# Moving loads, a small fold and the place of TensorE's instruction stream in a kernel that TensorE bounds

## The chip, the cores and the metric

The kernel runs on one core of a Trainium2 chip. The metric is the device time of one execution in microseconds (us). Engines are called PE (TensorE; its weight loads, PEld, are shown apart), DVE (VectorE), ACT (ScalarE), POOL (GpSimd) and SP (SyncE). L597 is line 597 of the kernel's source.

## The reference

Two steps, `mab` twice and then a two-layer network with a maximum. Four batches of 12,544 rows of 128 numbers go through both.

```python
def mab(q, kv):                       # attention, softmax over kv
    s = scale * (q @ kv.transpose(0, 2, 1))
    a = np.exp(s - s.max(-1, keepdims=True))
    a /= a.sum(-1, keepdims=True) + 1e-09
    return a @ kv
h = mab(I, x)                         # 32 inducing rows look at all of x
attn = mab(x, h)                      # all of x looks at the 32 rows of h
# then, with attn as rows of 128:
g = np.maximum(attn @ w1, attn @ w2)  # d_ff = 1024
out = g @ w_out
```

## The kernel before

The second `mab` and the network are fused. For each block of rows, PE makes the scores against `h`, ACT takes exp (tile `e2`), and **bursts** of eight small matmuls multiply it with `hwd` = h·(w2 - w1). DVE and ACT clip the results at zero into `relu`. **Finals**, 16 matmuls each, multiply `relu` with `w_out`, and DVE divides by the softmax sums into an output tile. The program is one list of 196 bursts, 49 a batch; after each burst comes one final, then whatever jobs are due at that burst:

```python
for g, (p, u) in enumerate(seq):
    # (cut: lead = opening products of two finals)
    p.burst(u, lead)                  # 8 matmuls, L597, and their evictions
    # (cut)
    for blk in stages.get(g, ()):
        blk.stage()                   # scores of a block that comes soon
    if queue:
        part, *a = queue.pop(0)
        part.final(*a)                # 16 matmuls, L659; every other one stores 256 KB
    # (cut: dens)
    for f, *a in jobs.pop(g, ()):
        f(*a)
```

The jobs of a batch prepare the next one: load its x, transpose it by DMA, make its scores and sums piece by piece (`p1_scores`, `p1_accum`), and at the end close the sum. `E`, the exponentials of the first `mab`, is summed into `eacc` on POOL, folded from 16 pieces to one, and PE adds it over the partitions:

```python
def small_fold(b):                    # four adds on POOL
    acc = st[b]["eacc"]
    n = P1B // 2
    while n:
        nc.gpsimd.tensor_add(out=acc[:, 0:n, :], in0=acc[:, 0:n, :], in1=acc[:, n : 2 * n, :])
        n //= 2
    st[b]["esum"] = acc[:, 0, :]

def small_h(b):                       # L413: the matmul that waits for it
    es = st[b]["esum"]
    bi, ps = bank([128, 512])
    nc.tensor.matmul(out=ps[:, 0:M], lhsT=ones32, rhs=es, start=True, stop=True)
    # (cut: DVE: reciprocal, hT4)

for b in range(B - 1):
    nb, g = b + 1, first[b]
    t0, l0 = (9, 24) if b == 0 else (-3, 16)
    at(g + t0, transpose_batch, nb)
    if nb + 1 < B:
        at(g + l0, hold_loads, nb)
    for i in range(NP1):              # 7 pieces
        s = g + (14 + 4 * i if b == 0 else 5 + 5 * i)
        at(s, p1_scores, nb, i)
        at(s + 2, p1_accum, nb, i)
        if nb + 1 < B:
            at(g + l0 + 3 * i, load_x, nb + 1, i)
    for s, f in ((41, small_fold), (43, small_h), (44, small_hwd), (45, small_m1)):
        at(g + s, f, nb)
```

POOL issues the loads (`load_x`) and most stores, and in its timeline the fold comes behind the store that the program puts ahead of it: in the profile before, at batch 2, that store went out at 169.85 us after 2.29 us of idle time that DVE ended, and the fold started at 170.41.

The softmax here doesn't subtract the row's maximum and nothing guards it: scores larger than these inputs give would overflow.

## Time and profile before

| | |
|---|---|
| time, 3 runs before the prediction | 341.23 us median (341.05 to 341.43) |
| profiled span | 339.1 us |
| PE busy | 329.4 us, 97% |
| DVE, ACT, POOL busy | 300.8, 270.7, 94.7 us |
| idle time of PE's matmuls over 0.15 us, after 40 us | 0.82, 0.76 and 0.76 us |

How to read it: PE is the engine that sets the time (97% busy, and 88% of the chain that ended last), so a microsecond counts only if it is taken from PE's own row. The prediction below shows the lines that lead to the three gaps. Two more ways of reading are used throughout:

- *Idle time with no releaser.* The profile ends a gap with the name of what released it. "<-issue" means that it found nothing. On a weight load, 0.2 to 0.4 us of "issue" is common here and cost nothing: in the profile before it stands 95 times ahead of the finals' weight loads (L659), 21.3 us in all and 0.4 at most, while their matmuls had no idle time (0.0 us).
- *Counting instructions.* Weight loads, matmuls and the few semaphore instructions of PE, counted in order of time, give each one its number. Whether two odd places are a multiple of 256 apart is then a subtraction. The 256 comes from the profile before: queue q8, which the page calls "instruction", moved 49 packets of 16,384 bytes, and PE's 12,646 records make 49.4 groups of 256. A packet that starts behind one crossing is read as holding what PE runs from the next crossing on: the two stalls of that profile ended 1.2 and 1.5 us after the end of packets that had started 3.7 and 4.4 us behind the crossings before them.

### The profile page before, as it was taken

To read this page: it belongs to the slowest core of one execution; us is meant where nothing else is said; L and a number is where in the kernel's file an instruction comes from. 1 tells how busy PE (TensorE), PEld (TensorE's weight loads), DVE (VectorE), ACT (ScalarE), POOL (GpSimd) and SP (SyncE) were. 2 spreads that over 40 slices of the span, in tenths; PEclk is the share of its full clock that TensorE was granted. 3 is DMA by queue.
4 is the path that set the end of the run, shared out by engine and by line. 5 is a ranking of instruction groups with operands and counts; after the bars stand their busy time and mean duration, and the time that the engine had idled before them with its cause. 6 is when DMAs were issued, how large, how long until landed. Compare 5 with 4: busy or idle time off the path is not lost.

```text
span 339.1 us, 14460 instructions
## 1 busy us (share of the span) xinstructions
PE 329.4 (97%) x6316; PEld 262.1 (77%) x6316; DVE 300.8 (89%) x634; ACT 270.7 (80%) x521; POOL 94.7 (28%) x166
## 2 busy tenths in 40 slices
PE   8999999999999999999999999999999999999995
PEld 3676788887878878888867878888767778878875
DVE  1669999999889999999988999999989998999993
ACT  3749878767898887888888877787879989888881
POOL 6332122437641233444242232333142100000000
PEclk9999999999999999999999999999999999999999
DMA  8999999999939985888319993221221221222223
GB/s 214 207 208 212 187 211 269 232 245 179 193 116 205 234 198 139 187 183 192 110 64 151 250 195 120 95 95 65 96 96 66 96 108 65 98 96 95 96 95 110
DMA packets 54143, 51.47 MB, mean 152 GB/s; under 512 B 41536, under 2 KB 42464, under 8 KB 54080
## 3 DMA queue, kind: packets, MB, share of 16 engines
q0 software_dynamic: 11552, 32.38, 38.1%
q1 hardware_dynamic: 42528, 18.17, 26.2%
q8 instruction: 49, 0.80, 1.0%
q14 instruction: 14, 0.11, 0.1%
HBM read 28.33 MB, written 25.69 MB: 159 GB/s over the span
## 4 chain that ended last, share of the span: by engine, by line
PE 88%; DVE 3%; DMA 3%; POOL 2%; ACT 2%; issue 1%; POOLq 0%
PE ps L659 55%; PE ps L597 19%; PE ps L612 4%; DMA xn<-in_x_dram 3%; PE ps L379 2%; PE ps L357 2%; PE ps L532 2%; ACT relu L632 1%; DVE relu L628 1%; DVE o L685 1%; POOL eacc L406 1%; PE ps L239 1%; PE ps L553 0%; PE ps L293 0%; PE ps L473 0%
## 5 line engine op out<-in xcount | busy, mean ns | idle before, releaser
L632 ACT ACTIVATE relu<-ps 128x512 f16<-128x512 f32 x443 | 234.6, 601 | 45.3 <-PE ps L597 30.8
L628 DVE TENSOR_SCALAR relu<-ps 128x512 f16<-128x512 f32 x341 | 219.6, 680 | 5.1 <-PE ps L597 4.2
L659 PE MATMUL ps<-woutp,relu 128*128 128x128 f16 x3136 | 208.7, 220 | 0.0
L659 PEld LDWEIGHTS <-relu 128*128 128x128 f16 x3136 | 175.7, 98 | 31.2 <-issue 21.3
L685 DVE TENSOR_TENSOR o<-ps,rp 128x256 f32<-128x256 f32 x196 | 82.0, 419 | 16.1 <-PE ps L659 11.2
L695 POOL DMA_DIRECT2D out_dram<-o x75 | 41.3, 551 | 156.7 <-DVE o L685 109.5
L597 PE MATMUL ps<-e,hwd 32*128 32x256 f16 (+1 forms) x1632 | 83.1, 268 | 1.6 <-issue 0.8
L597 PEld LDWEIGHTS <-hwd 32*128 32x128 f16 x1632 | 27.1, 92 | 20.7 <-issue 5.0
L612 PE MATMUL ps<-m,e 32*128 32x128 f16 x372 | 29.8, 214 | 0.7
L612 PEld LDWEIGHTS <-e 32*128 32x128 f16 x372 | 18.3, 92 | 6.8 <-issue 4.4
L399 POOL TENSOR_TENSOR eacc<-eacc,et 128x512 f32<-128x512 f32 (+1 forms) x18 | 18.5, 1030 | 0.3
L366 ACT ACTIVATE et<-ps 128x512 f16<-128x512 f32 (+1 forms) x21 | 11.4, 544 | 5.0 <-PE ps L357 5.0
L120 POOL DMA_DIRECT2D xn<-in_x_dram x21 | 11.4, 544 | 4.5 <-DMA xn<-in_x_dram 2.3
L542 ACT ACTIVATE e<-ps 128x512 f16<-128x512 f32 (+1 forms) x21 | 10.8, 568 | 0.0
L357 PE MATMUL ps<-inducingT,xT 128*128 128x32 f16 x294 | 10.6, 176 | 0.0
L379 PE MATMUL ps<-et,xn 128*128 128x32 f16 x294 | 10.6, 176 | 0.0
L357 PEld LDWEIGHTS <-xT 128*128 128x128 f16 x294 | 9.6, 96 | 0.0
L379 PEld LDWEIGHTS <-xn 128*128 128x128 f16 x294 | 9.5, 96 | 0.0
L532 PE MATMUL ps<-xT,hT 128*32 128x512 f16 (+2 forms) x120 | 8.7, 350 | 0.0
L191 PE MATMUL ps<-warm 128*128 128x512 f16 x22 | 7.4, 478 | 1.2 <-DVE warm L167 1.2
L239 PE MATMUL ps<-identity,xn 128*128 128x128 f16 x98 | 7.1, 219 | 0.6 <-DVE mask L726 0.3
L244 DVE COPY xT<-ps 128x1024 f16<-128x1024 f16 (+2 forms) x10 | 5.7, 585 | 1.4 <-PE ps L239 1.4
(84 smaller groups left out, 121.5 us busy)
## 6 DMA issues: line engine op xcount, KB each, us to landing
out_dram<-o POOLq DMA_DIRECT2D x72, 256.0 KB, 4.1
xn<-in_x_dram POOLq DMA_DIRECT2D x21, 512.0 KB, 8.5
out_dram<-o SPq DMA_DIRECT2D x24, 256.0 KB, 2.0
xf<-in_x_dram SPq DMA_DIRECT2D x2, 512.0 KB, 4.1
wf<-in_moe_w_dram SPq DMA_DIRECT2D x2, 512.0 KB, 5.0
xn<-in_x_dram POOLq DMA_DIRECT2D x3, 256.0 KB, 10.9
out_dram<-o POOLq DMA_DIRECT2D x3, 128.0 KB, 5.7
xT<-xn SPq DMA_TRANSPOSE x21, 7.0
```

Of the source, the lines that this page charges most:

```text
L120: nc.gpsimd.dma_start(out=xn_of(b, i)[:, 0:n, :], in_=xr[b, :, k0 : k0 + n, :])
L357: nc.tensor.matmul(out=ps[:, j * M : (j + 1) * M], lhsT=xT_tiles[b % 2][:, k0 + j, :], rhs=inducingT, start=True, stop=True,)
L379: nc.tensor.matmul(out=ps[:, 0:M], lhsT=xn[:, j, :], rhs=et[:, j, :], start=(j == 0), stop=(j == n - 1),)
L399: nc.gpsimd.tensor_add(out=acc, in0=acc, in1=et[:, 0:n, :])
L532: nc.tensor.matmul(out=ps[32 * q : 32 * (q + 1), 0 : self.width], lhsT=st[self.b]["hT4"][:, 32 * q : 32 * (q + 1)], rhs=xT[:, q % self.g], ...
L597: nc.tensor.matmul(out=ps[:, jj * w : (jj + 1) * w], lhsT=st[blk.b]["hwd"][r, 128 * jb : 128 * (jb + 1)], rhs=blk.e2[r, 128 * self.t0 : 12 ...
L612: nc.tensor.matmul(out=part.fin[q][1][:, 128 * s : 128 * (s + 1)], lhsT=part.blk.e2[r, 128 * tt : 128 * (tt + 1)], rhs=st[part.blk.b]["m1" ...
L628: nc.vector.tensor_scalar(out=dst, in0=src, scalar1=0.0, scalar2=None, op0=ALU.max)
L632: nc.scalar.activation(out=dst, in_=src, func=AF.Relu)
L659: nc.tensor.matmul(out=o, lhsT=self.relu[:, jb, q, tt, :], rhs=woutp[:, jb, :], start=(start and s == 0 and jb == 0), stop=(not start and ...
L685: nc.vector.tensor_mul(self.osb[:, h : h + 2, :], ps[:, 0:256].rearrange("p (s c) -> p s c", s=2), rp.broadcast_to((128, 2, 128)),)
L695: eng.dma_start(out=outr[blk.b, :, k : k + nst, :], in_=self.osb[:, 0:nst, :])
```

## The change

Its intent: end the loading of a batch sooner, take the fold of E out from behind a store, and put PE's instructions at a chosen place in the blocks in which they are fetched.

```diff
-                    at(g + l0 + 3 * i, load_x, nb + 1, i)
-            for s, f in ((41, small_fold), (43, small_h), (44, small_hwd), (45, small_m1)):
+                    at(g + l0 + 2 * i, load_x, nb + 1, i)
+            d = 1 if b == 0 else 0
+            for s, f in ((40, small_fold), (42 + d, small_h), (43 + d, small_hwd), (44 + d, small_m1)):
                 at(g + s, f, nb)
@@
         queue = []
+        nfinal = 0
@@
             if queue:
+                if nfinal == 4:
+
+                    nc.tensor.addr_align(256, offset=174, max_nops=0)
+                nfinal += 1
                 part, *a = queue.pop(0)
                 part.final(*a)
```

`addr_align(256, offset=174, max_nops=0)` asks that the next instruction lie at slot 174 of a block of 256.

## The prediction

> **What bounds the kernel now.** I read the page's busy rows first, then the waits, then the timeline at the places that the waits name. The page:

> ```profile
> span 339.1 us, 14460 instructions
> PE 329.4 (97%) x6316; PEld 262.1 (77%) x6316; DVE 300.8 (89%) x634; ACT 270.7 (80%) x521; POOL 94.7 (28%) x166
> ...
> PE   8999999999999999999999999999999999999995
> ...
> DMA  8999999999939985888319993221221221222223
> ...
> q8 instruction: 49, 0.80, 1.0%
> ```

> TensorE (PE) is busy in 97% of the span, and the slices show no hole of half a slice between the start and the last slice. The chain that ended last is 88% PE. So time can come only from PE: less work for it, which the change doesn't bring (its order of instructions gains one entry, the alignment), or fewer stalls. The DMA row shows two stretches of near full load, up to about 165 us, and light load after. I went through PE's matmuls in order and looked for idle time over 0.15 us. From 40 us to the end there are three: 0.82 us at 83.80, 0.76 at 172.47 and 0.76 at 251.30. The timeline shows what they are. The last two look alike; here is the second of them and, for comparison, the same place one batch earlier, where nothing waits:

> ```profile
> 91.53 1.99 POOL L406 TENSOR_TENSOR eacc<-eacc 128x256 f32<-128x256 f32 x4
> ...
> 93.77 0.30 PEld L413 LDWEIGHTS ps<-eacc,ones 128*128 128x128 f32 x2
> ...
> 169.85 0.54 POOL L695 DMA_DIRECT2D out_dram<-o  x1 [2.29 <-DVE o L685]
> ...
> 170.41 2.00 POOL L406 TENSOR_TENSOR eacc<-eacc 128x256 f32<-128x256 f32 x4
> ...
> 172.47 0.41 PE L413 MATMUL ps<-eacc,ones 128*128 128x32 f32 x2 [0.76 <-POOL eacc L406]
> ```

> The fold of E takes GpSimd (POOL) 2.0 us. At 170 us it stands in POOL's queue behind an output store that waits for VectorE (DVE), so it starts at 170.41 and PE waits for it. In the first batch it ends at 93.52 and PE comes at 93.77: no wait.

> The stall at 83.80 has no releaser. It falls inside a burst of eight matmuls, between the seventh and the eighth, where nothing in the program can differ:

> ```profile
> 82.59 0.39 PE L597 MATMUL ps<-e,hwd 32*128 32x256 f16 x7
> ...
> 83.80 0.09 PEld L597 LDWEIGHTS <-hwd 32*128 32x128 f16 x1 [1.10 <-issue]
> ...
> 83.80 0.28 PE L597 MATMUL ps<-e,hwd 32*128 32x256 f16 x1 [0.82 <-issue]
> ```

> A smaller one of the same look, also before the eighth of a burst, is in the weight loads at 70.86:

> ```profile
> 70.38 0.12 PEld L597 LDWEIGHTS <-hwd 32*128 32x128 f16 x7
> 70.86 0.09 PEld L597 LDWEIGHTS <-hwd 32*128 32x128 f16 x1 [0.36 <-issue]
> ```

> [...] With boundaries every 256 counted from these two, a fetch packet starts at or after each crossing: at once (within 0.2 us) for most crossings after 210 us, where DMA is light, but 3.7, 3.7 and 4.4 us late at the crossings of 64.80, 70.86 and 76.95 us. The packet then takes 0.9 to 1.5 us, and the stalled instruction came 1.2 to 1.5 us after its end. So a fetch under load needs about 3.7 to 4.4 + 0.9 + 1.3 = 5.9 to 6.6 us, while PE uses a block up in 5.9 to 7 us. That is the whole margin.
> [...]

> **The change part by part.**
> 1. *Fold of E one burst sooner.* For batches 2 and 3 the fold and all that follows (h, hwd, m1) move one burst forward; for batch 1 the fold alone. POOL's order becomes: store issued at 167.00, then the fold, at about 167.56 to 169.56, instead of after the store at 169.85. The matmul on it moves from after the final products of one burst (171.7) to after those of the burst before, about 170.3. It finds its sum 0.7 us old: no wait. What is it worth? From burst to burst across it PE takes 172.81 - 170.31 = 2.50 us at batch 2 and 251.64 - 249.14 = 2.50 at batch 3; the undisturbed place of batch 1 takes 94.11 - 92.48 = 1.63. So 0.87 us each, **1.74 us** together. For batch 1 there is nothing to gain. Nothing else comes to wait there, I think: in batch 1 the reciprocal and hT come after the same matmul without PE waiting.
> 2. *Loads two bursts apart, not three.* It removes no instruction. A burst with its final products takes about 1.45 us, so a 512 KB load (as written) comes every 2.9 us, not 4.4. With stores of 256 KB per 2.9 us that is 177 + 88 = 265 KB/us, against 116 + 88 = 204 before. From 64 to 98 us the queues moved some 190 to 230 at a DMA share of 0.93 to 1.0. So the DMA is full already and the change shortens the loading (seven loads in 12 bursts instead of 18) by piling up a backlog. Nobody waits for these loads: POOL's little copy that asks for the last one, at 100.9 us and 178.9, shows no wait. By itself the part is worth **0**. Its effect on the fetches is the point: fewer crossings meet load, but those that do meet more.
> 3. *Alignment.* It stands ahead of the fifth group of final products, at 36.04 us in the trace before. By my count of boundaries that instruction sits at slot 104 of its block; it moves to 174, some 70 slots on, in the same block[...]. [...] All later boundaries come 70 instructions earlier. By the old clock the crossings are then at 62.87, 68.94, 75.50, 81.43 and 88.83 us, and the blocks between take 6.1, 6.6, 5.9, 6.3 (with the stall taken out) and 7.2 us. Stalls removed: 1.10 + 0.36 = **1.46 us**. Stalls that may come back: with a need of 5.9 to 6.6 us the 5.9 us block and the 6.3 us one can each lose some 0.3 us, and in the second loading stretch (130 to 165 us), where waits were 0 to 2 us, denser loads may bring a little. I put **+0.8 us** for all of them.

> Sum: -1.74 - 1.46 + 0.8 + 0.1 = -2.3 us. 341.23 - 2.3 = **338.9 us**, 0.7% less.

> **The rivals.**
> *Fetch stalls return elsewhere.* For it: DMA share is at its limit, and in 130 to 165 us loads now come as densely as in the first stretch, with blocks of 6.0 to 6.4 us. Five to eight crossings meet load; at 0.3 to 1 us for half of them it gives back 1 to 3 us: 339.5 to 341. Against: the slot is a chosen one, most likely picked on a clock, and loading is over sooner.
> *Stores delayed by the backlog.* Stores share the loads' queue. They took 2.3 to 8.0 us to land in 64 to 98 us. Output tiles have four buffers, used again after about 4 x 2.9 = 11.6 us. A backlog of (265 - 210) x 17.6 = 970 KB at 210 KB/us is 4.6 us more, some 10 to 12 us at worst. Then DVE would wait for a buffer and PE for DVE: 0.5 to 2 us, once per stretch. Against: the backlog peaks only at the last loads.
> *Evictions take PE's place.* DVE is busy 9.2 to 9.6 us in most windows of 10 us. If the removed stalls only let DVE catch up, part of the 3.2 us returns as waits on evictions. Against: at batch 1, with no stall at the fold, PE ran through at 1.63 us. I allow 0.5 us.
> [...]

> **Range and chances.** If all works and no stall returns: 341.23 - 3.2 = 338.0; a little below if small stalls that I didn't count go too: low end 337.2. If the fold alone pays and stalls come back in full plus a store wait: 341.2. I take 337.2 to 341.2. Two per cent is 6.8 us, over twice all that can be removed, so faster has 1%; slower needs a new wait of 9 us, 1%.

> **What would show it right or wrong.** Fold: the wait of L413 on L406 is gone and PE takes about 1.6 us from burst to burst there. Fetch: no idle time with no releaser at the old places, boundaries shifted by about 70 instructions, late packets' waits still near 4 us while loads run. Loads: seven issues in some 18 us, landing later than 8.5 us after issue. Stores: DVE's products L685 waiting for an output DMA would prove the second rival; new idle time of PE with no releaser every 256 instructions the first. The prediction is wrong if POOL's earlier fold meets a blocked queue[...] or if the alignment costs more than a branch.

The sum came to -2.3 us and 338.9 us, as it stands. Its term of +0.1 us is for the alignment's branch; no trace of the kernel before shows a branch there. Without that term the sum is -2.4 us, 338.8 us.

## The result, and the profile after

| | before | changed |
|---|---|---|
| median, 6 runs each | 341.14 us (340.38 to 342.05) | 338.41 us (337.88 to 338.78) |
| ratio | | 0.9917, 95% interval 0.9899 to 0.9935 |
| profiled span | 339.1 us | 336.1 us |

The ratio is the mean time of one kernel's runs over that of the other's of the same rounds, so it isn't quite the ratio of the medians. The change is real and small, 2.7 us. The results agree with the reference.

The page of the changed kernel, its busy rows and the DMA rows:

```profile
span 336.1 us, 14462 instructions
...
PE 328.1 (98%) x6316; PEld 261.8 (78%) x6316; DVE 299.0 (89%) x632; ACT 271.6 (81%) x523; POOL 94.4 (28%) x166
...
DMA  8999899999629986993229992221221322222222
...
q8 instruction: 49, 0.80, 1.0%
```

PE has the same 6316 matmuls and still sets the time. Its busy time fell by 1.3 us and the span by 3.0; the ledger below shows that what went is stalls. Here is the place of the fold, batch 2, in the changed kernel's timeline (start, duration, engine, line, what, and in brackets the engine's idle time before it):

```profile
165.76 0.56 POOL L695 DMA_DIRECT2D out_dram<-o  x1 [2.13 <-DVE o L685]
...
166.34 2.00 POOL L406 TENSOR_TENSOR eacc<-eacc 128x256 f32<-128x256 f32 x4
...
168.07 1.07 PE L659 MATMUL ps<-woutp,relu 128*128 128x128 f16 x16
168.61 0.56 POOL L695 DMA_DIRECT2D out_dram<-o  x1 [0.27 <-DVE o L685]
168.92 0.30 PEld L413 LDWEIGHTS ps<-eacc,ones 128*128 128x128 f32 x2
168.97 0.36 PE L413 MATMUL ps<-eacc,ones 128*128 128x32 f32 x2
```

The fold starts right after the earlier store and ends at 168.34. PE comes for it at 168.92, after its final, and has no idle time. The next store comes after it in the queue and isn't held up: POOL is idle for 0.27 us until DVE has its tile ready.

And the place of the stall at 83.80 us, in the burst that starts at 82.59 us before and at 82.38 in the changed kernel:

```profile
82.37 0.12 PEld L597 LDWEIGHTS <-hwd 32*128 32x128 f16 x8
82.38 0.40 PE L597 MATMUL ps<-e,hwd 32*128 32x256 f16 x8
82.50 0.26 PEld L612 LDWEIGHTS <-e 32*128 32x128 f16 x4
```

All eight of the burst run together; there were seven and one.

**The ledger.** Take the same instruction in both timelines and subtract. The first final after the alignment starts at 36.04 us before and 36.18 in the changed kernel: +0.14. That difference is there from the first burst on (24.48 and 24.65 us), before any part of the change acts. The first burst after the new weights of batch 1 stands in the two timelines at:

```profile
95.87 0.12 PEld L597 LDWEIGHTS <-hwd 32*128 32x128 f16 x8 [0.42 <-issue]
```

```profile
94.61 0.12 PEld L597 LDWEIGHTS <-hwd 32*128 32x128 f16 x8 [0.42 <-issue]
```

That is -1.26, so 1.40 us went between 36 and 95 us: the two stalls with no releaser. Behind the fold of batch 2 the difference is -2.13 (the final at 177.60 is at 175.47), behind that of batch 3 -3.00 (256.43 and 253.43): 0.87 us each. From there to the end it stays -3.00. Fetch 1.40 + folds 1.74 - start 0.14 = 3.0 us, which is the whole difference of the spans.

### The profile page after: what moved, and what is told of

It reads as the page before. It is cut to its first block, busy times and chain, and to the rows that moved or that the text cites. A ratio compares the mean times of both kernels' runs of the same rounds, so it can differ in the third digit from the quotient of the medians.

```text
span 336.1 us, 14462 instructions
## 1 busy us (share of the span) xinstructions
PE 328.1 (98%) x6316; PEld 261.8 (78%) x6316; DVE 299.0 (89%) x632; ACT 271.6 (81%) x523; POOL 94.4 (28%) x166
## 4 chain that ended last, share of the span: by engine, by line
PE 91%; DMA 3%; ACT 2%; DVE 2%; issue 1%; POOL 1%; POOLq 0%
PE ps L659 58%; PE ps L597 19%; PE ps L612 4%; DMA xn<-in_x_dram 3%; PE ps L379 2%; PE ps L357 2%; PE ps L532 2%; ACT relu L632 1%; PE ps L239 1%; DVE o L685 1%; PE ps L553 1%; DVE relu L628 1%; PE ps L293 0%; PE ps L473 0%; DVE xT L244 0%
## 5 line engine op out<-in xcount | busy, mean ns | idle before, releaser
L685 DVE TENSOR_TENSOR o<-ps,rp 128x256 f32<-128x256 f32 x196 | 82.0, 418 | 16.5 <-PE ps L659 11.9
L695 POOL DMA_DIRECT2D out_dram<-o x75 | 41.2, 549 | 151.9 <-DVE o L685 102.9
L597 PE MATMUL ps<-e,hwd 32*128 32x256 f16 (+1 forms) x1632 | 82.4, 268 | 0.7 <-ACT relu L632 0.2
L597 PEld LDWEIGHTS <-hwd 32*128 32x128 f16 x1632 | 26.9, 92 | 19.1 <-issue 3.5
L379 PEld LDWEIGHTS <-xn 128*128 128x128 f16 x294 | 9.5, 96 | 0.0
L239 PEld LDWEIGHTS <-xn 128*128 128x128 f16 x98 | 5.8, 97 | 1.8 <-DMA xn<-in_x_dram 1.3
```

The source lines that it names most:

```text
L239: nc.tensor.transpose(ps[:, j, :], xn[:, g + j, :], identity16)
L379: nc.tensor.matmul(out=ps[:, 0:M], lhsT=xn[:, j, :], rhs=et[:, j, :], start=(j == 0), stop=(j == n - 1),)
L597: nc.tensor.matmul(out=ps[:, jj * w : (jj + 1) * w], lhsT=st[blk.b]["hwd"][r, 128 * jb : 128 * (jb + 1)], rhs=blk.e2[r, 128 * self.t0 : 12 ...
L685: nc.vector.tensor_mul(self.osb[:, h : h + 2, :], ps[:, 0:256].rearrange("p (s c) -> p s c", s=2), rp.broadcast_to((128, 2, 128)),)
L695: eng.dma_start(out=outr[blk.b, :, k : k + nst, :], in_=self.osb[:, 0:nst, :])
```

## The experiments

The questions: what does each part do alone; are the stalls with no releaser really instruction fetches that wait behind the loads; and is it the alignment or the spacing of the loads that removes them? There were twelve experiments. The first eight are shown with what they told; the last four put the open comparison into the same rounds, three of them as repeats. "Stall" below means idle time of PE's weight loads with no releaser, over 0.25 us, at a block boundary (a boundary's place is counted in instructions from 2498 and 3010, those of the two stalls before).

### Fold alone

The changed kernel with `3 * i` for the loads again and without the alignment.

> The fold of E one burst sooner, alone; loads three bursts apart and no alignment, as in the kernel before. Theory (two separate stalls): the two waits of the h matmul for GpSimd's fold, 0.87 us each, go, and nothing else: about 339.4 us if before is 341.14 (-1.7, ratio 0.995). The stalls with no releaser at about 70.9 and 83.8 us stay, at the same two instructions, since neither the instruction count before them nor the loads change. Rival (the evictions take the stall's place, or the fold only helps with earlier loads): under 0.7 us gained, and new waits of TensorE on VectorE or ScalarE after the fold.

Median 339.59 us (338.56 to 340.59, 4 runs) beside 340.99 of before; ratio 0.9967, 0.9928 to 1.0005; span 336.8. Both waits for the fold are gone. The stall at 70.9 us is there again, at the same instruction, and a little larger:

```profile
71.36 0.09 PEld L597 LDWEIGHTS <-hwd 32*128 32x128 f16 x1 [0.59 <-issue]
```

But the other, at 83.8 us, isn't, in a kernel whose program up to there is that of the kernel before. So the theory holds for the fold in the profile, and misses on one point: which fetch comes late differs from run to run. The timed runs alone don't settle it, since the interval just includes no gain. The four runs say so as well: two at 338.6 to 338.7, two at 340.4 to 340.6.

### Loads alone

The kernel before with `2 * i`.

> Loads two bursts apart, alone. Theory (fetch under load): block boundaries stay where they were, loads get denser, so stalls with no releaser remain in the first loading stretch, somewhere at the boundaries of 70.9, 77 and 83.8 us, 0.3 to 1.5 us together, and the time is within 1 us of before (340.3 to 342). Rival (the spacing alone cures the fetch, because loading is over sooner): all such stalls gone, -1.4 us, 339.7 us. The fold's two waits of 0.76 us stay in either.

Median 340.96 us (340.34 to 341.31), ratio 1.0005, 0.9978 to 1.0032; span 339.1. The fold's waits stay. The stalls stay too, at other boundaries of the same grid, 2754 and 3010 instead of 2498 and 3010; this is the first of them:

```profile
77.64 0.28 PEld L659 LDWEIGHTS <-relu 128*128 128x128 f16 x5 [0.66 <-issue]
```

With the 0.44 us of the second that makes 1.10 us, against 1.46 before. Spacing alone cures nothing: the theory, not the rival.

### Alignment alone

The kernel before with the alignment.

> The alignment alone, loads three apart, fold as before. Theory (boundaries moved by 70 instructions meet the loads at other moments): the stalls at the old two instructions go; if any come at the new boundaries they stand 70 instructions before the old ones plus multiples of 256. I expect 0 to 0.5 us of them, so -1.0 to -1.4 us: 339.7 to 340.1 us. Rival (the alignment does nothing without denser loads): stalls of 1.4 us remain, 341.1 us. [...]

Median 339.63 us (339.54 to 340.80), ratio 0.9976, 0.9946 to 1.0005; span 337.8. No stall over 0.25 us; at two of the new boundaries, 87.6 and 94.7 us, PE lost some 0.2 us and less. The fold's two waits of 0.75 us are there. The median lies just below the theory's 339.7 to 340.1. One run of four took 340.80, though, and the interval just includes no gain.

### Fold and loads, no alignment

The changed kernel without the alignment.

> The changed kernel without its alignment. If the alignment is what removes the fetch stalls: 1.0 to 1.5 us slower than the changed kernel (339.4 to 339.9 us), with a stall with no releaser inside the first loading stretch. If the spacing removes them: the same as the changed kernel, 338.4 us, and no such stall.

Median 338.67 us (338.19 to 339.28), ratio 0.9939, 0.9905 to 0.9972; span 337.1, against 336.1 with the alignment. The weight loads show where the microsecond is; it is the pattern of the run with the loads alone:

```profile
77.46 0.28 PEld L659 LDWEIGHTS <-relu 128*128 128x128 f16 x5 [0.66 <-issue]
...
83.65 0.09 PEld L597 LDWEIGHTS <-hwd 32*128 32x128 f16 x1 [0.44 <-issue]
```

The two stalls of the profile make 1.1 us, and the stalls are what the first of the two expectations had. The time isn't: that was 339.4 to 339.9 us, and 338.67 (mean 338.70) is nearer to the 338.4 of the other.

### The loads' traffic taken away

The kernel before with six of batch 2's seven loads left out, and the one that is left (i = 2) put where the last was. Its output is wrong, which doesn't matter for the time.

```diff
-                if nb + 1 < B:
-                    at(g + l0 + 3 * i, load_x, nb + 1, i)
+                if nb + 1 < B and (b > 0 or i == 2):
+                    at(g + l0 + (3 * i if b > 0 else 18), load_x, nb + 1, i)
```

> The kernel before with six of the seven loads of batch 2 left out (its result is wrong on purpose; the seventh load comes at the place of the last). Theory (the stalls at 70.9 and 83.8 us are instruction fetches that wait behind the loads' transfers): with the loads gone both stalls vanish, the late fetch packets between 70 and 92 us start under 2 us after their crossing instead of 3.3 to 4.4, and the time falls by about 1.4 us, to 339.6; the fold's two waits of 0.76 us stay. Rival (something at these instructions themselves, a bank or a wait that the profile does not name): the stalls stay.

Median 340.46 us (339.98 to 341.52), ratio 0.9994, 0.9957 to 1.0030; span 339.0. The time missed the expectation: 339.6 us was for a kernel before at 341, and beside the 340.30 of its own rounds nothing was gained. What bears the mechanism out is the profile alone. Windows of the stretch in question, the kernel before first (columns: the window, its length, busy us of PE, PEld, DVE, ACT and POOL with counts, granted clock, DMA share, GB/s):

```profile
72.00:80.00 8.00, 8.00 (x181) 6.87 (x179) 7.56 (x17) 5.68 (x11) 4.26 (x7) 1.00 0.95 201
80.00:88.00 8.00, 7.18 (x141) 5.67 (x139) 6.84 (x14) 6.04 (x14) 4.57 (x7) 1.00 0.91 193
```

The same windows without the loads:

```profile
72.00:80.00 8.00, 8.00 (x181) 6.86 (x179) 7.88 (x18) 5.94 (x12) 3.51 (x6) 1.00 0.28 102
80.00:88.00 8.00, 8.00 (x162) 6.48 (x160) 7.49 (x17) 7.07 (x15) 4.91 (x7) 1.00 0.23 83
```

DMA fell from over 0.9 to under 0.3, and PE's hole in 80 to 88 us is closed. The fetch packets (q8) that follow the crossings of 70, 77 and 83 us start 0.4, 0.1 and 0.2 us after them; before it was 3.7, 4.4 and 1.1 us. Both stalls are gone: at the first burst after the new weights this kernel stands at 94.93 us, where the kernel before is at 95.87. Since stalls come and go, one profile without them could be luck; but all five profiles with these loads and no alignment (before, the fold alone, the loads alone, fold and loads twice) have at least one of 0.36 to 1.10 us at these boundaries. What ate the gain in this profile was elsewhere. One part is a gap of 0.41 us at 45.7 us, in the weight loads of the new batch's scores, where a transpose ended the wait of the matmul. The other is this:

```profile
201.95 0.11 PEld L532 LDWEIGHTS <-hT 128*32 128x32 f16 x5 [0.71 <-issue]
```

That instruction is number 7617 or 7618 in the count, 5120 = 20 x 256 from 2498: a fetch again, late 4.3 us while the DMA transposes of the last batch were under way (DMA share 1.12 from 195 to 200 us). The kernel before had no stall there in its profile, and this kernel's program there is the same. So loads are one cause of late fetches here and not the only one, and which ones come late differed between these two executions.

### Three other slots

The changed kernel with `offset=110`, `206` and `238`.

> The changed kernel with slot 110 instead of 174: the boundaries come within six instructions of where they lie without alignment. Theory (only the place of the boundaries counts, the added entry itself is free): the stalls of the kernel without alignment come back, about 1.1 us in all near 77.5 and 83.6 us, six instructions earlier, so a profiled span of about 337.1 us against 336.1 and a time of about 339 us. Rival (the alignment helps in itself[...]): no stalls, 338.4 us.

> The changed kernel with slot 206: boundaries 32 instructions earlier than in the changed kernel. The blocks that meet the loads would take 5.92, 5.87 and 6.38 us from 68.6 us on. A fetch under load needs 5.9 to 6.6 us, so I expect 0.2 to 1.0 us of stalls at the ends of the first two, exactly at the new boundaries: 338.6 to 339.4 us. If no stall comes, the margin is wider than I think, and 174 is not special.

> The changed kernel with slot 238: boundaries 64 instructions earlier than in the changed kernel; blocks of 5.89, 5.92 and 6.43 us from 67.7 us on. Same reasoning: 0.2 to 1.0 us of stalls at the new boundaries, 338.6 to 339.4 us. If no stall comes, most slots are as good as 174 and only the natural one is bad.

| slot | boundaries against slot 174 | span | median (range), 4 runs | ratio to before | stalls in the profile |
|---|---|---|---|---|---|
| 110 | 64 later | 336.5 | 338.71 (338.25 to 339.89) | 0.9943 (0.9907 to 0.9980) | none |
| 206 | 32 earlier | 336.2 | 338.01 (337.91 to 338.08) | 0.9917 (0.9886 to 0.9948) | none over 0.15 us |
| 238 | 64 earlier | 336.8 | 338.50 (338.43 to 338.67) | 0.9931 (0.9894 to 0.9968) | 0.49 us at 37.2 us |

Slot 110 puts the boundaries back to within six instructions of where they lie without alignment, and the profile shows no stall where that build had 1.10 us: the expectation failed. Its fetches waited 1.9 to 3.1 us where those of the build without alignment waited 3.5 to 4.3. One of its four runs took 339.89. For slots 206 and 238, 0.2 to 1.0 us of stalls were expected where the loads run, and none came in these profiles: the margin was wider than I thought. Slot 206 had two fetches with next to no margin (1.51 and 1.44 us between the end of the packet and the first instruction of the block; where PE stood still this was 1.2 to 1.6 us) and no loss. Slot 238 lost time at a place that I hadn't considered, right behind the alignment:

```profile
36.33 0.38 PEld L659 LDWEIGHTS <-relu 128*128 128x128 f16 x6
37.20 0.39 PEld L659 LDWEIGHTS <-relu 128*128 128x128 f16 x7 [0.49 <-issue]
```

The jump from slot 104 to slot 238 leaves the block with 122 used instructions instead of 256. PE used it up in some 4.5 us (32.2 to 36.7). The packet of the next block had started 2.5 us after the crossing and ended at 35.65, 1.1 us before PE was there; PE went on 1.55 us after that end. So this jump, over 134 slots, was not free.

### The open comparison, in the same rounds

After eight runs the parts had been compared across three sets of rounds, in which the kernel before had medians from 340.30 to 341.14 us. So four kernels ran on one chip with five rounds each: the changed kernel, slot 206, the changed kernel with the loads three bursts apart, and the changed kernel without the alignment.

> The changed kernel once more, so that its parts can be compared on one chip in the same rounds. Profiles so far: no stall with no releaser in it, every late fetch with 1.7 us or more between the end of its packet and the first instruction of its block. 338.2 to 338.5 us, runs within 1 us of each other, where the kernel before spreads over 2 to 2.5 us.

> Slot 206 once more. Its four runs lay within 0.2 us (337.91 to 338.08). If that is the slot's doing, it repeats: 338.0 us, spread under 0.4 us, 0.1 to 0.5 us faster than slot 174. If it was the chip of that session, it is equal to slot 174 within 0.2 us.

> The changed kernel with its loads three bursts apart again (fold and alignment kept). If the spacing matters to the fetches: the crossings of 81 and 88 us are served as late as with the alignment alone (waits of 4.2 and 4.8 us, about 0.2 us lost), so 0.2 to 0.7 us slower than the changed kernel, 338.6 to 339.1, with more spread. If not: equal to it within 0.2 us.

> The changed kernel without its alignment once more. Its profile lost 1.1 us to late fetches, but a build with the boundaries six instructions away lost none, so the loss comes and goes from run to run. If the alignment is worth what that one profile says: 1 us slower than the changed kernel, 339.4. If the loss comes in only part of the runs: 0.3 to 0.6 us slower, 338.7 to 339.0, with runs spread over 1 us or more.

| kernel, 6 runs each (before: 11) | median | mean | range | ratio to before, 95% interval |
|---|---|---|---|---|
| before | 340.08 | 340.37 | 339.64 to 341.75 | |
| changed | 337.89 | 338.03 | 337.80 to 338.72 | 0.9931 (0.9908 to 0.9955) |
| slot 206 | 338.37 | 338.48 | 338.10 to 339.23 | 0.9945 (0.9923 to 0.9967) |
| fold and alignment | 338.24 | 338.42 | 337.82 to 339.16 | 0.9943 (0.9920 to 0.9966) |
| fold and loads | 338.50 | 338.88 | 338.16 to 340.01 | 0.9956 (0.9930 to 0.9983) |

The small spread of slot 206 didn't repeat, nor its lead over slot 174: in its profile one of the two fetches without margin came late this time.

```profile
80.73 0.10 PEld L597 LDWEIGHTS <-hwd 32*128 32x128 f16 x3 [0.26 <-issue]
```

Without the alignment the profile has one stall, 0.65 us, at the boundary of 2498, where the first profile of the same build had its stalls at 2754 and 3010. Neither the changed kernel nor fold and alignment show one in these rounds.

Against the changed kernel's mean, taking the alignment away cost 0.85 us and taking the loads' spacing away 0.39 us. The intervals of all four ratios overlap, so these two sizes are not settled. Of the expectations, the changed kernel came in under its 338.2 to 338.5 us; fold and alignment lies between its two cases; fold and loads fits the second of its two, a loss in only part of the runs (mean 338.88, spread 1.85). What is settled is that the fold with either of the other two, or with both, gained about 1.5 us or more by the means of these rounds. No variant here beats the changed kernel.

## Why the prediction was right or wrong

The predicted 338.9 us with 337.2 to 341.2 held the measured 338.41 us, and "within 2%" was right. The gain was 2.7 us in the first comparison and 2.3 us by the means of the repeat, which is the predicted sum to 0.1. That closeness is in part luck, since two of its terms are sizes that differ from run to run. By its steps:

**Fold, -1.74 us: right, to the hundredth.** From burst to burst across the h matmul PE took 1.64 us in the changed kernel (167.63 to 169.27) where I took 1.63 from batch 1 as the undisturbed case. The ledger has 0.87 us for each of the two batches. The fold alone gave 1.4 us in the medians, with fetch stalls blurring it, so the size rests on the profiles.

**Stalls with no releaser, -1.46 us removed: right in this profile (1.40), but a single draw.** I took one profile's stalls for the kernel's. They come and go: the same program up to 84 us showed 0.36 and 1.10 us in one profile and 0.59 us alone in another; the kernel before ranged over 1.7 to 2.6 us within one set of rounds, the changed kernel at most 0.9. By the profiles the alignment does help: one or two stalls of 0.36 us and more in each of the five without it that have these loads, none over 0.25 us in the four at slot 174. That they are fetches behind other DMA traffic is shown: every such stall stood at a multiple of 256 from the others of its build; those at slots 206 and 238 stood on the grid that the jump had set; without the loads the packets came within 0.4 us of the crossings and both stalls went. Most crossings lose nothing: after 36 us PE used a block up in 5.8 to 8.3 us in the profiles before and after the change, and of the 45 crossings in the one before, two held its weight loads up for over 0.25 us.

**Stalls that may come back, +0.8 us: the term that was mis-sized.** The profile of the changed kernel has none, and that more than covers the gap between 338.9 and 338.4. I computed them with a fetch's wait under load of 3.7 to 4.4 us. In the changed kernel the waits in the loading stretch were 2.7, 3.3 and 3.5 us, and the shortest margin 1.7 us. The repeat showed the same (at most 3.6 us). With the same boundaries but the loads three bursts apart, the waits at those four crossings (69 to 88 us) were longer: 3.4 to 4.8 us with the alignment alone and 2.9 to 3.7 with fold and alignment, against 1.4 to 3.5 and 1.1 to 3.6 with two apart. Denser loads don't shorten every wait: without the alignment, the fetches at the crossings of 136 to 148 us waited 2.4 to 3.9 us with loads two bursts apart and at most 1.9 with three, though PE lost next to nothing there. So at the same crossings the waits differed with the spacing of the loads, in both directions; by what rule stays open, and at slot 110 the waits were short too (1.9 to 3.1 us).

**Alignment's branch, +0.1 us (no trace had shown it): nothing to see.** From the burst ahead of it to the final behind it PE takes 0.33 us in both kernels (35.71 to 36.04, and 35.85 to 36.18). The branch itself is on record:

```profile
L849 PEldq COMPARE_BRANCH  x1: 187/187/187, 35.8 to 35.8; - x1
```

It took 187 ns, longer than the 0.1 us of the sum, while PE was at work on the burst ahead of it.

**Loads, worth 0 by themselves: right** (ratio 1.0005 alone). Beside the fold they may be worth something: by the means 0.9 us between the fold alone and fold and loads, 0.4 between fold and alignment and the changed kernel; neither is settled. My reading of the DMA was wrong, though, in two places. The light load after 165 us isn't all light: in the page's own row the slices from 178 to 203 us are full (a DMA share of 1.09), with the transposes of the last batch, and that is where the run without the loads had its late fetch. And I took the 190 to 230 KB/us of the first stretch for the most that the DMA can do, though the kernel before moved 275 in 64 to 72 us. These are the windows of the changed kernel:

```profile
72.00:80.00 8.00, 8.00 (x178) 6.87 (x175) 7.89 (x18) 5.93 (x13) 4.64 (x8) 1.00 1.05 247
80.00:88.00 8.00, 8.00 (x163) 6.48 (x160) 7.50 (x18) 7.05 (x16) 5.76 (x9) 1.00 1.05 236
88.00:96.00 8.00, 8.00 (x144) 6.29 (x142) 7.44 (x18) 7.36 (x15) 3.73 (x8) 1.00 0.29 104
```

It moved 247 and 236 GB/s where it had moved 201 and 193 at a share of 0.95 and 0.91. A share over 0.9 was not the limit. The last load lands at about 90 us instead of 98.

**The rivals.** *Fetch stalls elsewhere*: did not come in the changed kernel's two profiles, but did in its neighbours (slot 206 repeated, slot 238), so the rival was alive. *Stores delayed by a backlog*: fell with the DMA reading; stores in 64 to 98 us landed 6.3 us after issue at most, where I feared 10 to 12, and 8.0 before. *Evictions take PE's place*: no; the ledger loses nothing between the stalls. And at slot 238 came a stall that none of these names: PE's weight loads stood still for 0.49 us at the end of the block that the jump had left with 122 instructions.

**What stays open.** How much of the gain in time is the alignment's, how much the spacing's: their intervals overlap. Whether slot 174 is better than its neighbours, beyond chance. And why slot 110, whose boundaries lie almost where they lie without the alignment, had no stall in its one profile: that the alignment helps by itself is not ruled out, though slots 206 and 238 had stalls with it in place (0.26 us in the repeat, and 0.49).

## What to carry to other kernels

When one engine is busy 97% of the time, list its idle gaps in order of time and ask of each who released it; here three gaps and a short weight-load stall held the whole gain, and a small job moved ahead of a waiting store in POOL's order gave the most reliable part of it (0.87 us at each of two batches). A gap with no releaser in the middle of identical instructions is a reason to count instructions: here such gaps lay a multiple of 256 apart, they were late instruction fetches, and with the loads' traffic taken away the fetches came in time (0.1 to 0.4 us after the crossings where it had been 1.1 to 4.4). These stalls came and went from execution to execution, so judge a cure by the spread of many runs and not by one profile.
